# An adaLN transformer block on one core: W_o products of the first last tokens ahead of output sums, VectorE passes over two neighbouring banks, and the plan's constants set anew

## The chip, the cores and the metric

The kernel runs on one core of a Trainium2 chip. A core has five engines with instruction streams of their own: TensorE (PE, matrix products), VectorE (DVE), ScalarE (ACT, exponentials and GELU), GpSimd (POOL) and SyncE (SP, which here only issues DMA transfers). They wait for each other through semaphores; each works its own stream off in order. TensorE writes its results into PSUM, eight banks of 128 partitions x 512 fp32 columns. The metric is the device time of one execution in microseconds, lower is better. Of several executions the median is given.

## The reference, cut to what matters

One sequence of 2048 tokens, width 512, 32 heads of 16, a feed-forward width of 1376:

```python
mod = (silu(c) @ w_mod).reshape(...)                  # sa, ca, ga, sb, cb, gb
h = layernorm(x) * (1 + ca) + sa
q, k, v = split(h @ wqkv)                             # 32 heads of 16
p = softmax(q @ k.T * 16 ** -0.5)
x = x + ga * ((p @ v) @ wo)
h = layernorm(x) * (1 + cb) + sb
x = x + gb * (gelu(h @ w1 + b1) @ w2 + b2)
```

The bulk is attention: for each head 2048 x 2048 scores, their exponentials, and the sums of these with v.

## The kernel before, in words

**Tiling.** A unit of attention `qi` (32 of them) is one block of 512 query tokens, one chunk of eight heads, and one half of these heads, four at a time; the last four units (`halved`) take two halves of 256 tokens instead. A unit has 16 key tiles of 128 keys, and a key tile has four rows (heads): one row is a score product of 32 x 128 by 32 x 512 (`qk`, L922) into one bank. `order` lists all (unit, key tile) pairs, 512 in number.

**Two ways to an exponential.** ScalarE takes two rows at once from banks 0 and 1 (tile `pA`) or 3 and 4 (`pB`), L1291. Some of the key tiles (those listed in `DKT`) go to VectorE and GpSimd instead: VectorE adds a constant to the score and writes int16 (`p_pass`, L1362), a number whose bits read as fp16 are already close to 2**score; three more copies of the tile (`emit_shift`), shifted by constants, are made on VectorE (L1333) or GpSimd (L1339), and products with scaled copies of v (`VV`) sum the four into a better exponential. These rows use the four banks 2, 5, 6 and 7 (`flex`), which they share with output sums and with all other products (`jobs`). A tile of this kind costs four passes, three shifts and 16 products of output sums where ScalarE's way costs two exponentials and four.

**Output sums.** `pv_issue` (L1086) issues a group of four products, one for each row and 32 columns of TensorE; in the halved units the group is eight products of 256 columns. When a unit's sums are complete, VectorE copies them out (L1398), a chain of small DMAs brings the denominators to where they are needed (SP queue: L1419, L1427, L1455, L1465), and GpSimd multiplies (L1477) into `OT`.

**The plan.** The order of all engines' instructions is written out by a planner inside the kernel, when it is built: it keeps a clock for each engine with a price for each kind of work, takes the engine whose clock is lowest, and asks `pe`, `act`, `dve` or `pool` what to issue. Its choices hang on constants. `jobs` (products into a free bank, then an evacuation) and `tasks` (work of another engine) become due when the position in `order` reaches their gate: projections of k and q (`K_GATE`, `Q_GATE`), W_o products (`X1_GATE`), the first and second feed-forward product of a block (`U_GATE`, `OUT_GATE`; `U2_GATE`, `OUT2_GATE` for the third block). `D_AHEAD` and `D_WAIT` say how early and with how much room before the next score group TensorE may issue rows for VectorE alone, `OPEN_N` how many finished exponentials a unit's sums need before they get a bank, `POOL_MIN` how much other work VectorE must have before GpSimd takes a shift, `D_STOP` how many key tiles of a unit must be left. `X_LEAD` moves the position that gates see. `TURNS` sets such constants for one of 64 turns, a turn being half a unit. Time does not enter when the kernel runs: only the order and the semaphores do.

`pe` asks in turn: scores for ScalarE, a bank for a unit's sums, rows for VectorE, then either a step of an open job (`px`) or a group of sums (`pf`) if it ends before the next scores are due. L1191 decides between the last two.

**The end.** For the last block of 512 tokens the first 256 are handled early: the jobs `xA` (eight W_o products for each of the two token tiles) make the residual, then statistics on VectorE (L281, L286), a root on GpSimd (L291, L292), the norm (L782), and two transposing DMAs (L509) into `ha`. For the other 256 tokens the jobs `z` issue the W_o products of three of the four head chunks (`Z_GATE` says when); the fourth follows when the last unit is done. After the last exponential `last_tail` writes a fixed order: VectorE's chain for the last unit (from L1634), with the feed-forward products of the first 256 tokens (L668) as fillers between its steps. `GAPS` says how many fillers go into each gap.

Of the kernel before, what the change touches and what calls it, by code (L numbers as in the profile page):

```python
# [34 lines left out]
VOFF = 16  # L35
VEW = VOFF + H * HS + 16

TURNS = {29: {'D_AHEAD': 0.3}, 30: {'D_AHEAD': 0.3}, 31: {'D_AHEAD': 0.3}, 32: {'D_AHEAD': 0.3}, 47: {'OPEN_N': 10}, 48: {'OPEN_N': 10}, 60: {'D_STOP': 5}, 61: {'D_STOP': 5}, 62: {'D_STOP': 5}, 63: {'D_STOP': 5}}
TURN = 2
DKT = (3, 7, 11, 13, 14, 15)  # L40
NV = 4
# [3 lines left out]
T_BUFS = 5  # L45
P_BUFS = 5
D_FROM = 0
D_AHEAD = 0.1
D_STOP = 4

INF = 1e18
# [30 lines left out]
START = 11.4  # L82
WARM = (16, 0, 0)
Q_POOL = False
PAIR = False
K_GATE = (-1.7, 0.25)
Q_GATE = -1.1
X1_GATE = (0.3, 1.3)
U_GATE = (1.7, 5.0)
OUT_GATE = (5.0, 7.9)  # L90
OPEN_N = 14
LN1_DMA = (2, 3)
LN2_DMA = True
# [1 line left out]
POOL_MIN = 1.0  # L95
D_WAIT = 0.5
# [1 line left out]
TIE = True  # L98
SEARCH = None
NARROW = False  # L100
GAPS = (10, 4, 0, 12, 2, 3, 8, 4)
NHQ = 4
N2_ENG = DV
NHC = NC - NHQ // 2
MMH = 0.25
SP_DH = (0.5, 1.75)
XA_AT = 30.5
U2_GATE = (1.7, 5.0)
OUT2_GATE = (4.6, 7.2)
LOAD_AT = (2, 3)  # L110
D_END = 6
BULK_LEFT = 8
Z_GATE = 0.2


def bf16_round(v):
# [47 lines left out]
def adaln_block(ctx: ExitStack, tc: tile.TileContext, A_x, A_wqkv, A_wo, B_x, B_w1, B_b1, B_w2, B_b2,  # L164
# [386 lines left out]
    for ch in range(1, NC):  # L551
        for b in range(NQB):
            add_k(ch, b, 2 * ch + K_GATE[0] + K_GATE[1] * b)
        add_q(ch, 0, 2 * ch + Q_GATE)
    for b in range(1, NQB):
        for ch in range(NC):
            add_q(ch, b, 8 * b + 2 * ch + Q_GATE)

# [126 lines left out]
    def add_tail(b):  # L685
# [35 lines left out]

        u_gate, out_gate = (U2_GATE, OUT2_GATE) if b == NQB - 2 else (U_GATE, OUT_GATE)
        for fc in range(NFC):
# [97 lines left out]
    st = {"ap": 0, "cur": None, "mode": None, "unit": 0, "lastpe": 0.0, "expd": 0, "extra": 0.0}  # L821

    V = dict(D_AHEAD=D_AHEAD, D_STOP=D_STOP, OPEN_N=OPEN_N, D_WAIT=D_WAIT, POOL_MIN=POOL_MIN, X_LEAD=0.0)
    base = dict(V)
    turn = [-1]

    def next_turn():

        n = st["ap"] * TURN // 16
        if n > turn[0]:  # L830
            turn[0] = n
            V.update(base)
            if SEARCH is not None:
                SEARCH(n, V)
            V.update(TURNS.get(n, {}))

# [33 lines left out]
    xopen = []  # L870
# [266 lines left out]
    def x_mode():  # L1137
        return xopen[0].mode
# [14 lines left out]
    def pe(now):  # L1153
        if issue_unit(now):
            return True
        if open_o(now):
            return True
        x_open(now)
        dl = INF
        if more_units():  # L1160
            u = st["unit"]
            tf = unit_free[u] if unit_free[u] < INF else max(T[AC], now) + EXP_BUSY[unit_cap[u]] + 0.16
            if tf > now:
                dl = max(tf, act_dry() - 0.56)

        def fits(dur, mode):
            return now + (SWITCH if mode != st["mode"] else 0.0) + dur <= dl + 0.03

        sel = pv_pick(now)
        full = len(sel) == 4  # L1170
        dve_idle = T[DV] + 0.6 * (len(dbanks) + sum(1 for x in evacs if x.ready < now + 0.3)) <= now + V["D_AHEAD"]
        if dve_idle and fits(MM, "row") and (dl - now > V["D_WAIT"] or T[DV] <= now and not dbanks):
            banks = bank_for_d(now)
            n = 0
            avoid = []
            while banks and n < 2 and want_d(now, len(banks)):
                r = d_next(now, avoid)
                if r is None:
                    break
                s = now + (SWITCH if st["mode"] != "row" else 0.0)  # L1180
                d_issue(r, s, banks.pop(0))
                avoid.append(r)
                n += 1
            if n:
                pe_start(now, "row", MM, "drow")
                return True
        px = bool(xopen) and fits(xopen[0].cost, x_mode())
        pf = full and fits(MM, "col")
        if not more_units():
            px = px and not pf  # L1190
        if px and not (pf and (pv_pressure() or (x_mode() == "full" and st["mode"] == "col" and not xopen[0].k))):  # L1191
            x_step(now)
            return True
        if pf:
            pv_issue(now, sel)
            return True
        if px:
            x_step(now)
            return True
        idle = now - st["lastpe"]  # L1200
        if sel and fits(MM, "col") and idle > 0.12:
            pressure = pv_pressure() or any(claimed[e[1]] == NKT for _, e in sel)
            if pressure:
                pv_issue(now, sel)
                return True
        if idle > 0.15 and fits(MM, "col") and fill(now):
            return True
        if idle > 0.3 and now > st["extra"] + 0.3:
            extra_fill(now)
        return False  # L1210
# [12 lines left out]
    def pv_pressure():  # L1223
        return any(sl.slots[sl.i][0] for sl in rings) or bool(ring_t.slots[ring_t.i][0]) \
            or bool(ring_u.slots[ring_u.i][0])
# [124 lines left out]
    def p_pass(now):  # L1350
# [3 lines left out]
        n = 1  # L1354
        if PAIR and dbanks and dbanks[0][0] <= now and dbanks[0][1] == i + 1 and dbanks[0][2] is d \
                and dbanks[0][3] == r + 1:
# [236 lines left out]
    def last_tail():  # L1593
# [46 lines left out]
        nc.vector.reciprocal(out=rt, in_=den)  # L1640
        gap(GAPS[0])
        for t in range(2):
# [12 lines left out]
        rs = ln_root(mv, 2)  # L1655
        gap(GAPS[3])
        hns = [otp.tile([P, 512], BF16, name="OT") for _ in range(2)]
# [195 lines left out]
```

## Time and profile before

| | |
|---|---|
| median of 3 runs | 746.65 us (746.38 to 748.83) |
| profiled execution | 745.1 us, span 743.1 us |
| busy: ScalarE, TensorE, VectorE, GpSimd | 717.6, 726.9, 681.9, 422.7 us |
| granted TensorE clock | 1.00 |
| first and last exponential's start | 13.04 and 716.17 us |
| exponentials / int16 passes / shifts on VectorE and GpSimd | 736 / 576 / 240 and 192 |

The span is the time from the first to the last instruction; the execution holds some microseconds around it. A group of instructions in the profile is given with its line, engine, operation, output and inputs, its count, its busy time and the mean of one in ns, and the idle time of its engine in front of it with what ended it. Busy times of matmuls and of ScalarE overlap with those of their neighbours. In the timeline the columns are start, length, and the instruction with its count; a bracket at the end tells the idle time before it.

### The profile page before, as it was taken

What the parts mean: (1) busy time and instruction counts of PE and PEld (TensorE: products, weight loads), DVE (VectorE), ACT (ScalarE), POOL (GpSimd) and SP (SyncE); (2) the same over time, 40 slices, a digit from 0 to 9 for tenths busy, and PEclk for the clock granted to TensorE, in tenths of its full rate; (3) what the DMA queues carried; (4) which work ended last, traced back from release to release, by engine and by line L of the source; (5) the groups of instructions that cost most, each with busy time, mean ns of one, the idle gap of its engine ahead of it and who ended that gap; (6) DMA issues with size and microseconds to landing.
All of it is one profiled execution on the core that took longest, in us unless ns stands there. A gap on an engine that the chain in (4) does not pass through costs nothing.

```text
span 743.1 us, 22093 instructions
## 1 busy us (share of the span) xinstructions
PE 726.9 (98%) x9043; PEld 237.0 (32%) x9046; DVE 681.9 (92%) x1188; ACT 717.6 (97%) x775; POOL 422.7 (57%) x263
## 2 busy tenths in 40 slices
PE   8999999999999999999999999999999999999998
PEld 3323323232333222222222222322232222434455
DVE  8958899999999999999999999999999999989973
ACT  4999999999999999999999999999999999999993
POOL 3102756766565566676777465765667668653610
PEclk9999999999999999999999999999999999999999
DMA  8600101021120100000100200000010200010110
GB/s 275 169 13 2 25 4 24 22 56 48 45 65 11 38 10 23 7 16 24 53 17 8 45 5 15 11 18 24 18 50 5 46 10 9 19 33 15 43 26 31
DMA packets 42859, 25.57 MB, mean 34 GB/s; under 512 B 27609, under 2 KB 37906, under 8 KB 42754
## 3 DMA queue, kind: packets, MB, share of 16 engines
q1 hardware_dynamic: 41938, 23.01, 11.9%
q8 instruction: 72, 1.18, 0.7%
q10 hardware_dynamic: 816, 1.12, 0.4%
q14 instruction: 33, 0.27, 0.1%
HBM read 16.58 MB, written 2.61 MB: 26 GB/s over the span
## 4 chain that ended last, share of the span: by engine, by line
ACT 49%; PE 37%; issue 9%; DVE 4%; POOL 1%; DMA 0%; SPq 0%; DVEq 0%; ACTq 0%; POOLq 0%
ACT pA L1291 24%; ACT pB L1291 24%; PE PS L1086 12%; PE PS L922 12%; PE PS L254 8%; PE PS L668 3%; DVE t L1333 1%; POOL t L1339 1%; DVE t L1362 1%; PE PS L259 1%; ACT uG L728 1%; DVE qm L341 1%; ACT L1291 0%; DMA hT<-OT 0%; PE PS L1103 0%
## 5 line engine op out<-in xcount | busy, mean ns | idle before, releaser
L1339 POOL TENSOR_SCALAR t<-t 128x2048 int16<-128x2048 int16 x192 | 363.7, 1901 | 242.9 <-DVE t L1333 108.9
L1291 ACT ACTIVATE pA<-PS 128x1024 bf16<-128x1024 f32 x368 | 396.0, 1076 | 2.5 <-PE PS L922 2.1
L1291 ACT ACTIVATE pB<-PS 128x1024 bf16<-128x1024 f32 x368 | 396.6, 1078 | 0.1
L1362 DVE TENSOR_SCALAR t<-PS 128x512 int16<-128x512 f32 x576 | 370.5, 680 | 26.1 <-PE PS L922 23.2
L922 PE MATMUL PS<-qm,kT 32*128 32x512 bf16 x2048 | 304.6, 383 | 6.9 <-ACT pA L1291 3.2
L1086 PE MATMUL PS<-t,VV 128*32 128x512 f16 (+1 forms) x1956 | 225.1, 359 | 2.4 <-POOL t L1339 2.1
L922 PEld LDWEIGHTS <-kT 32*128 32x128 bf16 x2048 | 86.4, 91 | 285.0 <-issue 281.0
L1333 DVE TENSOR_SCALAR t<-t 128x2048 int16<-128x2048 int16 x240 | 175.5, 757 | 0.5 <-PE PS L1086 0.2
L1086 PE MATMUL PS<-pA,VE 128*32 128x512 bf16 (+1 forms) x826 | 168.4, 361 | 0.0
L1086 PE MATMUL PS<-pB,VE 128*32 128x512 bf16 (+1 forms) x826 | 164.3, 361 | 0.0
L1086 PE MATMUL PS<-t,VE 128*32 128x512 f16 (+1 forms) x652 | 133.6, 359 | 1.0 <-DVE o_sb L1398 1.0
L1086 PEld LDWEIGHTS <-VE 128*32 128x32 bf16 x2304 | 70.1, 94 | 76.9 <-issue 71.7
L1086 PEld LDWEIGHTS <-VV 128*32 128x32 bf16 x1956 | 65.0, 95 | 59.5 <-issue 53.0
L254 PE MATMUL PS<-h2T,W 128*32 128x512 bf16 x528 | 42.8, 383 | 0.0
L254 PE MATMUL PS<-W,uG 128*32 128x512 bf16 x528 | 40.3, 383 | 0.0
L1103 PE MATMUL PS<-kT,zeros 128*32 128x512 bf16 x296 | 28.3, 383 | 0.0
L1477 POOL TENSOR_TENSOR OT<-o_sb,rb 128x512 bf16<-128x512 f32 (+1 forms) x17 | 20.0, 1177 | 13.3 <-DVE t L1333 11.6
L719 DVE TENSOR_SCALAR uG<-PS,b1c 128x512 bf16<-128x512 f32 x33 | 24.5, 741 | 1.6 <-PE PS L254 1.2
L291 POOL TENSOR_SCALAR rs<-mv 128x4 f32<-128x4 f32 (+1 forms) x10 | 4.3, 427 | 36.5 <-DVE mv L286 36.0
L341 DVE TENSOR_SCALAR qm<-PS,qmask 128x512 bf16<-128x512 f32 x32 | 22.6, 741 | 2.2 <-PE PS L254 2.2
L254 PE MATMUL PS<-hT,W_k 128*32 128x512 bf16 x256 | 21.2, 383 | 0.5 <-DVE hT L324 0.5
L254 PE MATMUL PS<-hT,W_q 128*32 128x512 bf16 x256 | 20.9, 383 | 0.0
(129 smaller groups left out, 365.1 us busy)
## 6 DMA issues: line engine op xcount, KB each, us to landing
rb<-d SPq DMA_DIRECT2D x112, 32.0 KB
W_m<-in_w_mod_dram SPq DMA_DIRECT2D x2, 1024.0 KB
out_dram<-ob SPq DMA_DIRECT2D x15, 128.0 KB
o_sb<-o SPq DMA_DIRECT2D x56, 32.0 KB
xb<-in_A_x_dram SPq DMA_DIRECT2D x3, 512.0 KB
xr<-in_A_x_dram SPq DMA_DIRECT2D x3, 512.0 KB
W<-in_B_w_dram SPq DMA_DIRECT2D x4, 344.0 KB
W<-in_B_w_dram SPq DMA_DIRECT2D x5, 256.0 KB
```

The costliest lines, as they stand in the source:

```text
L254: nc.tensor.matmul(out=ps[32 * g:32 * g + 32, :], lhsT=lhsT[:, 32 * g:32 * g + 32], rhs=rhs, start=start, stop=stop)
L341: nc.vector.tensor_scalar(out=qm[(b, ch)][:, par, :], in0=ps, scalar1=qmask[:, par:par + 1], scalar2=None, op0=ALU.mult)
L668: nc.tensor.matmul(out=ps, lhsT=lhsT, rhs=rhs, start=start, stop=stop)
L719: nc.vector.tensor_scalar(out=X["u"][:, fc, :], in0=bank(ps), scalar1=late["b1c"][:, fc:fc + 1], scalar2=None, op0=ALU.add)
L922: nc.tensor.matmul(out=dst, lhsT=kT[rows, ch, kt * P:(kt + 1) * P], rhs=rhs, start=True, stop=True)
L1086: nc.tensor.matmul(out=bank(O[qi])[32 * r:32 * r + 32, cs], lhsT=w, rhs=rhs[:, cs], start=(n == 1 and not halved(qi)), stop=last and (pr = ...
L1103: nc.tensor.matmul(out=bank(O[qi])[32 * r:32 * r + 32, :], lhsT=zeros[:, 0:32], rhs=kT[:, 0, 0:512], start=False, stop=False)
L1291: nc.scalar.activation(out=t[:, 0:n, :], in_=PS[:, b0:b0 + n, :], func=ACT.Exp, scale=math.log(2.0) / STEP)
L1333: nc.vector.tensor_scalar(out=t16[:, rs, :], in0=d["tile"][:, rs, :], scalar1=float(MJ[j]), scalar2=None, op0=ALU.add)
L1339: nc.gpsimd.tensor_scalar(out=t16[:, rs, :], in0=d["tile"][:, rs, :], scalar1=1.0, scalar2=float(MJ[j]), op0=ALU.mult, op1=ALU.add)
L1362: nc.vector.tensor_scalar(out=d["tile"][:, r:r + n, :], in0=PS[:, i:i + n, :], scalar1=T_BIAS, scalar2=0.0, op0=ALU.add, op1=ALU.max)
L1477: nc.gpsimd.tensor_tensor(out=ot[:, 0:w], in0=o[:, 0:w], in1=rb[:, 0:w], op=ALU.mult)
```

## The change

Three parts. L1191: a job `xA` that is open is no longer held back by a group of sums that is ready. `PAIR`: where two neighbouring rows of one tile lie ready in two neighbouring banks, `p_pass` takes both in one instruction of 1024 columns. And constants: gates, `D_AHEAD`, `GAPS`, `Z_GATE`, and another `TURNS` table.

```diff
-TURNS = {29: {'D_AHEAD': 0.3}, 30: {'D_AHEAD': 0.3}, 31: {'D_AHEAD': 0.3}, 32: {'D_AHEAD': 0.3}, 47: {'OPEN_N': 10}, 48: {'OPEN_N': 10}, 60: {'D_STOP': 5}, 61: {'D_STOP': 5}, 62: {'D_STOP': 5}, 63: {'D_STOP': 5}}
+TURNS = {17: {'D_WAIT': 0.8}, 18: {'D_WAIT': 0.8}, 19: {'D_WAIT': 0.8}, 20: {'D_WAIT': 0.8}, 45: {'D_AHEAD': 0.4}, 46: {'D_AHEAD': 0.4}, 37: {'X_LEAD': -0.1}, 38: {'X_LEAD': -0.1}, 39: {'X_LEAD': -0.1}, 40: {'X_LEAD': -0.1}, 55: {'D_WAIT': 0.7, 'OPEN_N': 16}, 56: {'D_WAIT': 0.7, 'POOL_MIN': 0.8, 'OPEN_N': 16}, 57: {'D_WAIT': 0.7}, 58: {'D_WAIT': 0.7, 'X_LEAD': 0.1}, 59: {'X_LEAD': 0.0}, 60: {'D_WAIT': 0.7, 'X_LEAD': 0.0}, 61: {'D_WAIT': 0.7, 'X_LEAD': 0.0}, 62: {'D_WAIT': 0.7, 'X_LEAD': 0.0}, 63: {'D_WAIT': 0.7}, 51: {'D_WAIT': 0.7}, 52: {'D_WAIT': 0.7}, 53: {'D_WAIT': 0.7}, 54: {'D_WAIT': 0.7}}
...
-D_AHEAD = 0.1
+D_AHEAD = 0.2
...
-PAIR = False
-K_GATE = (-1.7, 0.25)
-Q_GATE = -1.1
+PAIR = True
+K_GATE = (-1.7, 0.22)
+Q_GATE = -1.2
 X1_GATE = (0.3, 1.3)
-U_GATE = (1.7, 5.0)
-OUT_GATE = (5.0, 7.9)
+U_GATE = (1.7,4.8)
+OUT_GATE = (4.6, 7.8)
...
-GAPS = (10, 4, 0, 12, 2, 3, 8, 4)
+GAPS = (10, 4, 0, 12, 3, 3, 7, 4)
...
-U2_GATE = (1.7, 5.0)
-OUT2_GATE = (4.6, 7.2)
+U2_GATE = (1.7,4.6)
+OUT2_GATE = (4.6,7.4)
...
-Z_GATE = 0.2
+Z_GATE = 0.6
...
-        if px and not (pf and (pv_pressure() or (x_mode() == "full" and st["mode"] == "col" and not xopen[0].k))):
+        if px and (xopen[0].name[0] == "xA" or not (pf and (pv_pressure() or (x_mode() == "full" and st["mode"] == "col" and not xopen[0].k)))):
             x_step(now)
             return True
```

The line of `p_pass` that `PAIR` switches on stood in the kernel before:

```python
        if PAIR and dbanks and dbanks[0][0] <= now and dbanks[0][1] == i + 1 and dbanks[0][2] is d \
                and dbanks[0][3] == r + 1:
```

## The prediction

> **What bounds the kernel now.** I read the page's totals first, then the waits by engine, then busy time by stage, and last the timeline of ScalarE and TensorE. Page and waits (waited for: us in total, times, longest):
>
> ```profile
> span 743.1 us, 22093 instructions
> PE 726.9 (98%) x9043; PEld 237.0 (32%) x9046; DVE 681.9 (92%) x1188; ACT 717.6 (97%) x775; POOL 422.7 (57%) x263
> ...
> L1339 POOL TENSOR_SCALAR t<-t 128x2048 int16<-128x2048 int16 x192 | 363.7, 1901 | 242.9 <-DVE t L1333 108.9
> L1291 ACT ACTIVATE pA<-PS 128x1024 bf16<-128x1024 f32 x368 | 396.0, 1076 | 2.5 <-PE PS L922 2.1
> L1291 ACT ACTIVATE pB<-PS 128x1024 bf16<-128x1024 f32 x368 | 396.6, 1078 | 0.1
> ...
> L1362 DVE TENSOR_SCALAR t<-PS 128x512 int16<-128x512 f32 x576 | 370.5, 680 | 26.1 <-PE PS L922 23.2
> ```
> ```profile
> PE PS L922 <- ACT pA L1291: 3.2, 13, 0.6
> PE PS L1086 <- POOL t L1339: 2.1, 6, 0.5
> DVE t L1362 <- PE PS L922: 23.2, 63, 1.1
> ```
>
> ScalarE runs 736 exponentials of two 512-column tiles and hardly idles. The exponentials overlap, so the distance between their starts counts, not their 1.08 us. Stages: before the pause of the first GELU, the first and the last of three such pauses, and what follows the last exponential's start.
>
> ```profile
> 13.04:304.77 291.73, 288.16 (x3379) 87.10 (x3379) 267.28 (x479) 290.51 (x315) 156.02 (x98) 1.00 0.16 42
> 304.77:313.39 8.62, 7.51 (x100) 2.54 (x92) 8.37 (x14) 8.56 (x6) 5.89 (x4) 1.00 0.02 4
> ...
> 646.13:654.75 8.62, 8.22 (x167) 4.25 (x159) 8.40 (x13) 8.56 (x5) 4.27 (x3) 1.00 0.02 5
> ...
> 716.17:743.10 26.93, 23.11 (x171) 15.29 (x170) 12.26 (x30) 12.90 (x27) 0.94 (x2) 1.00 0.10 29
> ```
>
> The columns are length, then busy time of TensorE, its weight loads, VectorE, ScalarE and GpSimd. From the first exponential's start to the last one's are 716.17 - 13.04 = 703.13 us: 735 distances, three of them pauses of 8.62. What sets an ordinary distance stands in TensorE's timeline, here around one long one:
>
> ```profile
> 366.46 0.39 PE L922 MATMUL PS<-qm,kT 32*128 32x512 bf16 x3
> 366.79 0.39 PE L1086 MATMUL PS<-pA,VE 128*32 128x512 bf16 x2
> ...
> 367.01 0.38 PE L1086 MATMUL PS<-t,VE 128*32 128x512 f16 x1
> ...
> 367.23 0.38 PE L1086 MATMUL PS<-t,VE 128*32 128x512 f16 x1
> ...
> 367.55 0.39 PE L922 MATMUL PS<-qm,kT 32*128 32x512 bf16 x4
> ```
> ```profile
> 367.07 1.03 ACT L1291 ACTIVATE pA<-PS 128x1024 bf16<-128x1024 f32 x1
> 368.11 1.02 ACT L1291 ACTIVATE pB<-PS 128x1024 bf16<-128x1024 f32 x1
> 369.03 1.02 ACT L1291 ACTIVATE pA<-PS 128x1024 bf16<-128x1024 f32 x1
> ```
>
> Between two score groups (366.46, 367.55) lie three groups of output products 0.22 apart. The next exponential starts 0.56 after its scores, and the distance is 1.04; the following one is 0.92. I counted the groups between neighbouring score groups in the program's order and held them against all distances. The first and last with three groups, of 148 outside the pauses:
>
> ```profile
> 16.67 1.05 ACT L1291 ACTIVATE pA<-PS 128x1024 bf16<-128x1024 f32 x1
> 17.58 1.07 ACT L1291 ACTIVATE pB<-PS 128x1024 bf16<-128x1024 f32 x1
> ...
> 709.79 1.15 ACT L1291 ACTIVATE pA<-PS 128x1024 bf16<-128x1024 f32 x1
> 710.73 1.12 ACT L1291 ACTIVATE pB<-PS 128x1024 bf16<-128x1024 f32 x1
> ```
>
> These 148 average 0.971 (143.7 in all); the other 584 (a lone 2.06 near the start among them) average (703.13 - 25.86 - 143.7) / 584 = 0.914. So ScalarE bounds most of the span, and TensorE stretches it where three groups lie in one interval.
>
> **The change, part by part.** The retuned constants reorder the whole plan, so I price what its order contains, counted in the built program.
>
> *Exponentials.* 734 instead of 736: one more score tile goes the integer way (145 instead of 144; 580 rows instead of 576). Three-group intervals: 146 instead of 149 (one of the 149 lay in a pause). With the prices above: 25.86 + 146 x 0.971 + 584 x 0.914 = 701.4, against 703.1 from the same rounded prices: two ordinary-to-long distances less, -1.9. Against it, the three-group intervals hold more changes between TensorE's tile shapes: those with one, two, three changes number 15, 82, 49, where they were 36, 83, 30 and averaged 0.953, 0.971, 0.992. That mix costs +0.8 in full. Ends -1.9 and -1.1; I take -1.5, the middle, since the shape changes may only mark a crowded stretch.
>
> *The extra tile on the others.* Three more GpSimd tables (195 instead of 192) and three more half-width product groups, 0.23 each; GpSimd is 57% busy, and the groups are in the interval count. The zero products put into idle TensorE slots make 80 groups instead of 81. Nothing more is added to the sum; if the tables had no cover, they would cost GpSimd 3 x 1.9 us.
>
> *GpSimd's tables.* A late table delays products, then scores, then the exponential:
>
> ```profile
> 144.36 1.03 ACT L1291 ACTIVATE pB<-PS 128x1024 bf16<-128x1024 f32 x1
> 145.53 1.02 ACT L1291 ACTIVATE pA<-PS 128x1024 bf16<-128x1024 f32 x1
> ```
> ```profile
> 144.64 0.40 PE L1086 MATMUL PS<-t,VV 128*32 128x512 f16 x4 [0.20 <-POOL t L1339]
> ```
>
> That distance is 1.17, 0.26 above 0.91, and there are 6 such waits. In the new order 4 tables are first read within two exponentials of their issue, where 10 were. Ends 0 and -1.6 (all six gone); I take half, -0.8.
>
> *Passes over two banks.* 42 pairs replace 84 of the passes; 496 single ones stay. No pair is in this trace. Widths of VectorE reading scores' banks, and two passes back to back:
>
> ```profile
> 705.53 1.27 DVE L1362 TENSOR_SCALAR t<-PS 128x512 int16<-128x512 f32 x2
> ...
> 737.52 0.69 DVE L1691 TENSOR_TENSOR ob<-PS,xr 128x512 bf16<-128x512 f32 x1 [1.76 <-PE PS L668]
> 738.72 0.42 DVE L1691 TENSOR_TENSOR ob<-PS,xr 128x256 bf16<-128x256 f32 x1 [0.51 <-PE PS L668]
> ```
>
> 256 more elements cost 0.27, so a pair takes about 0.69 + 0.54 = 1.23 where two take 1.27: 42 x 0.04 = 1.7 us of VectorE at best, and 42 x 0.09 = 3.8 us more of it if a pair cost twice the mean single pass (1.36). I take 1.23, the row of one instruction. VectorE waits 23.2 us for scores already, so either is covered: 0 in the sum; without that cover it would be a gain of 1.7 or a loss of 3.8. What it can cost: the first row of a pair is handed over 0.54 later than by a single pass, and so is its bank, for which TensorE's next scores wait. By the row, the second bank comes at 1.23 instead of 1.27 and a tile's tables need all four rows anyway: 0.
>
> The Trainium skill, "PSUM — Partial Sum Buffer", section "PSUM bank collisions raise a hardware error", says to guard PSUM by bank and quadrant with semaphores: TensorE may not refill a bank while VectorE still reads the pair. No run here shows it for pairs; by the row the sum stays, by that rule it is that of the third rival below.
>
> *W_o products first.* The condition on L1191 puts the eight products of each of the two jobs ahead of output sums. By the order, the second result's add comes 9 exponentials before the last instead of 7; but four shift passes of about 0.6 now stand before the two normalisations, which come 4 and 3 before the last (5 and 4 before), and the two transposing DMAs 4 and 2 (both 4). On SP the x load of the last half moves from 20 to 9 exponentials before the last, ahead of the transposes; its issue takes 0.40 and the transposes come five exponentials later, so it holds nothing up; its data are needed only by the adds after the last exponential.
>
> ```profile
> 696.62 0.40 SPq L804 DMA_DIRECT2D xr<-in_A_x_dram  x1
> ```
>
> *Tail.* Rows of the end:
>
> ```profile
> 710.56 0.41 PE L1086 MATMUL PS<-t,VV 128*32 128x256 f16 x8
> 710.79 0.28 PE L1086 MATMUL PS<-pA,VE 128*32 128x256 bf16 x2
> ...
> 716.45 1.03 PE L668 MATMUL PS<-W_o,OT 128*128 128x512 bf16 x4 [0.16 <-issue]
> 717.40 0.29 PE L1086 MATMUL PS<-pA,VE 128*32 128x256 bf16 x2
> ...
> 718.31 2.54 PE L668 MATMUL PS<-hT,W 128*128 128x256 bf16 x20 [0.17 <-DMA hT<-OT]
> ...
> 726.63 0.59 PE L668 MATMUL PS<-W,hT 128*128 128x512 bf16 x2
> 727.36 1.91 PE L668 MATMUL PS<-h2T,W 128*128 128x256 bf16 x16
> ```
> ```profile
> 714.07 0.73 DVE L782 TENSOR_SCALAR OT<-hT,mv,rs 128x512 bf16<-128x512 bf16 x2 [0.92 <-POOL rs L292]
> ```
>
> From the last exponential's start TensorE is busy 23.11 of 26.93 us, so the end follows from when the feed-forward products start (718.31, after a wait of 0.17 for the transposes). The new order leaves 33 half-width output products behind the last scores instead of 13: 20 / 8 x 0.23 = +0.58; six W_o products stand there in both. Of that, 0.16 idle before 716.45 and the 0.17 wait absorb 0.33. The transposes: the statistics come two exponentials earlier, so the 0.92 wait for GpSimd goes, and three shift passes of 0.6 take its place; the second transpose lands at about the same time after the last exponential and is hidden under the later TensorE. The gaps' new filler (three products instead of two behind the transposes) goes into the 0.14 between 727.22 and 727.36. Ends 0 and +0.75; I take +0.3.
>
> *Sum.* -1.5 - 0.8 + 0.3 = -2.0: span 741.1, profiled execution 743.1 (its 745.1 holds 2.0 around the span). The median of the three runs is 1.55 above that execution; the prediction carries this over: 746.65 - 2.0 = 744.7. Its own range goes from -1.9 - 1.6 + 0 to -1.1 + 0 + 0.75: 743.1 to 746.3.
>
> **Rivals.** *The tail eats the gain.* Nothing of +0.58 is absorbed, three W_o products of 0.22 that used to run while TensorE waited for the last exponential now follow the sums (+0.66), the mix costs its full +0.8, and the tables' waits stay: -1.9 + 0.8 + 1.2 = +0.1, 746.8. For it: the order shows all of these. Against: the 0.33 of idle time is there.
>
> *Long intervals get cheaper.* 23 three-group intervals that follow one with a single group average 0.930. If half of the 146 go that way because TensorE is less late before them, 73 x 0.04 = 2.9 more: 741.8. Against: such pairs number 22 in the new order.
>
> *Pairs hand over late: slower.* TensorE works in order, so each wait for a pair's bank or first row costs ScalarE up to the 0.26 of a late table. The gain is gone at 8 of 42 pairs, no-change is left behind at 17 ((2.0 + 2.24) / 0.26); half of them give -2.0 + 21 x 0.26 = +3.5, 750.1. For it: VectorE's 63 waits for scores say banks are tight, and TensorE has little slack in long intervals. Against: passes first read within one exponential number 6, where 14 did.
>
> **How the numbers follow.** A measurement can tell about 0.3%, 2.24 us: faster is below 744.4, slower above 748.9. Forecast 0.40 (its range lies across 744.4: 0.18 faster, 0.22 same), tail 0.20 (same), cheaper intervals 0.17 (faster), late pairs 0.23 (slower). Faster 0.35, same 0.42, slower 0.23. The range 741.6 to 749.6 leaves out some 0.06 of the fast side and half of the late pairs.
>
> **What would show it.** Right: 734 exponentials, the last one starting near 714.2 to 714.7; pauses still 8.62; TensorE's waits for GpSimd at 3 or so; pairs near 1.2 us; feed-forward products starting about 2.4 us after the last exponential's start, with no wait for the transposes. Wrong: waits of TensorE's scores for VectorE's passes, distances above 1.1 after pairs, pairs well over 1.3 us, or pauses longer than 8.62 because the first sums' results come late.

## The result and the profile after

The changed kernel takes 744.5 us, median of 12 runs (743.42 to 746.97); the kernel before took 746.62 beside it (745.38 to 748.83, 12 runs). The ratio is 0.9971, 95% interval 0.9957 to 0.9985: 1.1 to 3.2 us less, about 2.2. The prediction had said 744.7. A second measurement of the same kernel gave 743.96 and 0.9976 [0.9964, 0.9987]. The profiled execution took 744.46, span 742.6.

The page of the kernel after: span, then two rows of engines' busy times, then groups of instructions.

```profile
span 742.6 us, 22110 instructions
PE 724.4 (98%) x9066; PEld 235.7 (32%) x9066; DVE 680.9 (92%) x1150; ACT 716.8 (97%) x773; POOL 429.4 (58%) x266
...
L1339 POOL TENSOR_SCALAR t<-t 128x2048 int16<-128x2048 int16 x195 | 369.1, 1901 | 238.7 <-DVE t L1333 124.0
L1291 ACT ACTIVATE pA<-PS 128x1024 bf16<-128x1024 f32 x367 | 393.6, 1073 | 2.2 <-PE PS L922 2.0
L1291 ACT ACTIVATE pB<-PS 128x1024 bf16<-128x1024 f32 x367 | 393.9, 1073 | 0.0
```

Its groups with the shapes apart, VectorE's passes:

```profile
L1362 DVE TENSOR_SCALAR t<-PS 128x512 int16<-128x512 f32 x496 | 321.5, 679 | 22.9 <-PE PS L922 20.0 <-issue 0.3
...
L1362 DVE TENSOR_SCALAR t<-PS 128x1024 int16<-128x1024 f32 x42 | 51.0, 1213 | 2.7 <-PE PS L922 2.2 <-issue 0.2
```

Its waits (in total, times, longest):

```profile
DVE t L1362 <- PE PS L922: 22.2, 52, 1.4
...
PE PS L922 <- ACT pB L1291: 3.9, 15, 1.0
...
PE PS L922 <- ACT pA L1291: 2.7, 10, 0.9
...
PE PS L1086 <- POOL t L1339: 1.5, 4, 0.8
...
PE PS L306 <- DMA W_m<-in_w_mod_dram: 0.8, 1, 0.8
```

Busy time by stage: up to the first pause, the first and last pause, and from the last exponential's start (columns as before).

```profile
13.94:303.23 289.29, 285.25 (x3355) 86.64 (x3355) 263.89 (x460) 288.04 (x312) 159.21 (x99) 1.00 0.16 41
303.23:311.78 8.55, 7.14 (x101) 2.64 (x97) 7.95 (x12) 8.49 (x6) 6.57 (x5) 1.00 0.01 3
644.17:652.77 8.60, 8.18 (x147) 3.85 (x138) 8.26 (x13) 8.55 (x5) 3.52 (x3) 1.00 0.03 8
715.89:742.60 26.71, 23.39 (x192) 15.53 (x182) 12.17 (x30) 12.97 (x27) 0.94 (x2) 0.99 0.10 28
```

The stages show what the ends of the execution hide. From the first exponential's start to the last one's are 715.89 - 13.94 = 701.95 us, 1.18 less than before; from there to the end 26.71 instead of 26.93, 0.2 less (the span is printed to 0.1 us, so the end is good to 0.05). Together that is 1.4. The 0.90 by which the first exponential comes later (13.94 against 13.04) is not the change's: it goes with the last wait above, for the load of `W_m` ahead of everything that was changed; two kernels below that differ from this one only later, after_split and after_oldgaps, begin at 13.04 and 13.12.

All distances between neighbouring exponentials' starts, in the classes of the prediction (three-group intervals; ordinary ones under 1.1; strays of 1.1 or more, without the 2.06 near the start, which stayed at 2.07), each as count, mean and sum:

| | before | after |
|---|---|---|
| three groups | 148, 0.971, 143.7 | 146, 0.976, 142.5 |
| ordinary | 577, 0.909, 524.5 | 581, 0.911, 529.3 |
| strays | 6, 1.171, 7.0 | 2, 1.167, 2.3 |
| three pauses | 25.84 | 25.70 |

Two distances fewer at the ordinary 0.909 are -1.82; what the three-group intervals take beyond 0.909 rose from 9.2 to 9.8, +0.63; the strays' excess fell by 1.05; and the ordinary distances, longer by 0.002 each, gave 1.19 back. With -0.14 from the pauses that is -1.18.

Do the strays that went away come from late tables of GpSimd? The kernel before has six waits of TensorE for such a table: the one at 144.64 that the prediction shows, and these.

```profile
480.11 0.40 PE L1086 MATMUL PS<-t,VV 128*32 128x512 f16 x4 [0.49 <-POOL t L1339]
482.88 0.40 PE L1086 MATMUL PS<-t,VV 128*32 128x512 f16 x4 [0.48 <-POOL t L1339]
495.75 0.40 PE L1086 MATMUL PS<-t,VV 128*32 128x512 f16 x4 [0.22 <-POOL t L1339]
585.15 0.40 PE L1086 MATMUL PS<-t,VV 128*32 128x512 f16 x4 [0.51 <-POOL t L1339]
649.51 0.30 PE L1086 MATMUL PS<-t,VV 128*32 128x256 f16 x4 [0.16 <-POOL t L1339]
```

Three of them lie in pauses (475.36 to 483.98 and 646.13 to 654.75), where ScalarE runs no exponentials, and the one at 495.75 has distances of 0.90 and 0.94 around it. Only two lie at a stray: 144.64 at 1.17 and 585.15 at 1.28. Together these two exceed 0.909 by 0.63. The other four strays hold no wait for a table. Of the four waits of the kernel after, two lie in pauses (310.06 and 476.81), and none lies at a stray.

The start of the end, from the last scores for ScalarE to the first feed-forward product, before and then after:

```profile
715.57:718.31 2.74, 2.41 (x19) 0.84 (x20) 0.40 (x1) 2.72 (x3) 0.10 (x1) 1.00 0.48 96
715.27:718.13 2.86, 2.86 (x44) 1.32 (x41) 0.50 (x1) 2.84 (x3) 0.00 (x0) 1.00 0.29 56
```

TensorE was idle for 0.33 of the 2.74 us, and for none of the 2.86. It is busy 0.45 us longer there, and the products start 0.1 later after the last exponential's start.

### The profile page after: what moved, and what is told of

It reads as the page before. It is cut to its first block, busy times and chain, and to the rows that moved or that the text cites. A ratio compares the mean times of both kernels' runs of the same rounds, so it can differ in the third digit from the quotient of the medians.

```text
span 742.6 us, 22110 instructions
## 1 busy us (share of the span) xinstructions
PE 724.4 (98%) x9066; PEld 235.7 (32%) x9066; DVE 680.9 (92%) x1150; ACT 716.8 (97%) x773; POOL 429.4 (58%) x266
## 3 DMA queue, kind: packets, MB, share of 16 engines
q10 hardware_dynamic: 816, 1.12, 0.4%
## 4 chain that ended last, share of the span: by engine, by line
ACT 48%; PE 39%; issue 8%; DVE 3%; DMA 1%; POOL 0%; ACTq 0%; POOLq 0%; DVEq 0%
ACT pB L1291 23%; ACT pA L1291 23%; PE PS L1086 14%; PE PS L922 13%; PE PS L254 9%; PE PS L668 2%; ACT uG L728 1%; DMA W_m<-in_w_mod_dram 1%; DVE t L1362 1%; DVE qm L341 0%; PE PS L1103 0%; ACT L1291 0%; DVE t L1333 0%; POOL t L1339 0%; DVE st L281 0%
## 5 line engine op out<-in xcount | busy, mean ns | idle before, releaser
L1339 POOL TENSOR_SCALAR t<-t 128x2048 int16<-128x2048 int16 x195 | 369.1, 1901 | 238.7 <-DVE t L1333 124.0
L1362 DVE TENSOR_SCALAR t<-PS 128x512 int16<-128x512 f32 (+1 forms) x538 | 369.9, 721 | 25.6 <-PE PS L922 22.2
L1086 PE MATMUL PS<-pA,VE 128*32 128x512 bf16 (+1 forms) x822 | 163.3, 362 | 0.0
L1086 PE MATMUL PS<-t,VE 128*32 128x512 f16 (+1 forms) x660 | 130.9, 357 | 0.0
L254 PE MATMUL PS<-W,uG 128*32 128x512 bf16 x528 | 42.5, 383 | 0.0
L1103 PE MATMUL PS<-kT,zeros 128*32 128x512 bf16 x320 | 30.5, 382 | 0.0
```

Source lines behind the costliest of these rows:

```text
L254: nc.tensor.matmul(out=ps[32 * g:32 * g + 32, :], lhsT=lhsT[:, 32 * g:32 * g + 32], rhs=rhs, start=start, stop=stop)
L1086: nc.tensor.matmul(out=bank(O[qi])[32 * r:32 * r + 32, cs], lhsT=w, rhs=rhs[:, cs], start=(n == 1 and not halved(qi)), stop=last and (pr = ...
L1103: nc.tensor.matmul(out=bank(O[qi])[32 * r:32 * r + 32, :], lhsT=zeros[:, 0:32], rhs=kT[:, 0, 0:512], start=False, stop=False)
L1339: nc.gpsimd.tensor_scalar(out=t16[:, rs, :], in0=d["tile"][:, rs, :], scalar1=1.0, scalar2=float(MJ[j]), op0=ALU.mult, op1=ALU.add)
L1362: nc.vector.tensor_scalar(out=d["tile"][:, r:r + n, :], in0=PS[:, i:i + n, :], scalar1=T_BIAS, scalar2=0.0, op0=ALU.add, op1=ALU.max)
```

## The experiments

The table holds what the profiles of all kernels show, in the terms that the experiments turn on: exponentials; from the first one's start to the last one's ("region"); and, after the last one's start, when the feed-forward products begin, when VectorE's last chain (L1634) begins, when TensorE's last products (`W,uG`) begin, and the end of the span (good to 0.05). Ratios are to the kernel before, measured beside each. The gates, `D_AHEAD` and `Z_GATE` were not set back by themselves, so what each of them is worth is not known.

| kernel | exponentials | region | products | L1634 | `W,uG` | end | median, ratio [95%] |
|---|---|---|---|---|---|---|---|
| before | 736 | 703.13 | 2.14 | 1.74 | 18.77 | 26.93 | 746.62 |
| after | 734 | 701.95 | 2.24 | 1.74 | 18.56 | 26.71 | 744.50, 0.9971 [0.9957, 0.9985] |
| after_again | 734 | 701.97 | 2.24 | 1.74 | 18.55 | 26.70 | 743.96, 0.9976 [0.9964, 0.9987] |
| after_split | 734 | 702.32 | 2.24 | 1.74 | 18.56 | 26.94 | 744.42, 0.9996 [0.9982, 1.0010] |
| after_oldcond | 734 | 701.96 | 3.31 | 1.73 | 19.35 | 27.53 | 745.17, 0.9995 [0.9982, 1.0007] |
| after_oldgaps | 734 | 701.98 | 2.24 | 1.74 | 18.77 | 27.00 | 744.19, 0.9982 [0.9967, 0.9996] |
| after_nopair | 740 | 707.90 | 2.72 | 1.52 | 18.74 | 27.19 | 749.95, 1.0054 [1.0040, 1.0068] |
| after_oldturns | 738 | 706.31 | 2.53 | 2.34 | 19.15 | 27.68 | 748.94, 1.0039 [1.0025, 1.0054] |
| after_noturns | 736 | 704.32 | 3.54 | 1.70 | 19.76 | 27.98 | 748.30, 1.0037 [1.0023, 1.0051] |
| after_dup12 | 746 | 715.38 | 2.25 | 1.76 | 18.57 | 27.01 | 756.20, 1.0133 [1.0110, 1.0155] |
| after_fill2 | 734 | 705.27 | 3.07 | 1.74 | 19.11 | 27.27 | 748.01, 1.0023 [1.0008, 1.0039] |
| before_xa | 736 | 703.13 | 2.39 | 2.51 | 19.54 | 27.74 | 746.44, 1.0008 [0.9991, 1.0025] |
| before_pair | 738 | 705.03 | 2.58 | 2.33 | 19.36 | 30.48 | 751.13, 1.0064 [1.0042, 1.0086] |
| before_pair_again | 738 | 704.73 | 2.69 | 2.33 | 19.36 | 30.76 | 752.10, 1.0091 [1.0075, 1.0108] |

### The same kernel again

No edit.

> The changed kernel once more, unchanged, beside the kernel before on one chip. The traces so far say that two executions differ in when the first load of w_mod lands (first exponential at 12.9 to 15.5 us), and that what follows repeats to about 0.1 us. My theory: first exponential's start to last one's 701.95 +- 0.1, tail 26.7 +- 0.1, whatever the first start; ratio to the kernel before 0.998 (1.4 us less from the first exponential on), within 0.9971 to 0.999. Rival (the gain of 2.1 us is all in what follows the first exponential): a ratio of 0.997 and a length below 701.5.

Region and end came out within 0.02 of the first execution. What differed is the start: the first exponential began at 16.43 instead of 13.94, and the waits of this execution name the load.

```profile
PE PS L306 <- DMA W_m<-in_w_mod_dram: 1.8, 1, 1.8
```

Over all kernels the first exponential began between 12.91 and 16.43. The region repeats within 0.02 us here and within 0.30 in the two executions of before_pair, so differences of the region above some 0.3 can be read; differences between the times of single executions cannot.

### The pairs, issued as singles in the same order

```diff
-        nc.vector.tensor_scalar(out=d["tile"][:, r:r + n, :], in0=PS[:, i:i + n, :], ...)
+        for x in range(n):
+            nc.vector.tensor_scalar(out=d["tile"][:, r + x, :], in0=PS[:, i + x, :], ...)
```

> The changed kernel with its whole order kept, but each of the 42 passes over two banks issued as two passes over one bank, back to back. My theory (VectorE is covered, ScalarE's exponentials and TensorE's long intervals set the time): the same time as the changed kernel, 744.5 +- 0.7; VectorE's busy time about 2 us longer (42 x (1.27 - 1.21)), TensorE's waits for VectorE's passes unchanged. Rival 1 (a pair hands its first row and bank over late): faster by up to 42 x 0.26 = 11 us, visibly at least 2 us, with fewer waits of scores for VectorE. Rival 2 (the pairs themselves bring the gain): slower by about 2 us, 746.6.

The region grew by 0.37 us, hardly more than two executions of one kernel can differ. The median, 744.42, is that of after (744.50, 743.96); the kernel before was at 745.23 beside it, so the ratio is 0.9996 where after's are 0.9971 and 0.9976, and the intervals just overlap. By the profile the pairs themselves bring 0.4 at most; the times leave room for more. The profile's groups after the edit:

```profile
L1363 DVE TENSOR_SCALAR t<-PS 128x512 int16<-128x512 f32 x580 | 372.2, 679 | 24.2 <-PE PS L922 21.5
```

VectorE is not relieved by them: 496 singles and 42 pairs take 321.5 + 51.0 = 372.5 us, 580 singles 372.2 (busy times overlap), not the 2 us more that was expected. The pairs do not hand over late by any amount that shows: without them the region is no shorter.

### The plan without pairs

```diff
-PAIR = True
+PAIR = False
```

> The changed kernel with PAIR off, so that the plan is made anew without two-bank passes: 740 exponentials instead of 734 and 137 three-group intervals instead of 146. My theory prices the order: (740 - 4 - 137) x 0.914 + 137 x 0.971 = 680.3, against 675.3 for the changed kernel by the same prices: +5.0, 749.5 +- 1. It says that pairs pay through the plan: VectorE's time that they free lets the planner give VectorE three more key tiles. Rival (pairs cost TensorE waits, so the plan without them runs closer to its order): 745 to 747. Rival (TensorE's total work bounds, fewer integer tiles mean fewer products): 742 or less.

+5.95 us in the region, 1.0054 in time. The planner prices a pair at 1.135 us and two singles at 2 x 0.602, and the order that it makes with pairs sends three more key tiles to VectorE, each of which otherwise costs ScalarE two exponentials: 740 exponentials without pairs, 734 with them. So nearly all that the pairs bring in this plan comes through the order, although VectorE itself is not relieved by them. The region grew by 0.95 more than the count of exponentials and three-group intervals gives (+5.0).

### The former `TURNS`, and none

```diff
-TURNS = {17: {'D_WAIT': 0.8}, ... 54: {'D_WAIT': 0.7}}
+TURNS = {29: {'D_AHEAD': 0.3}, ... 63: {'D_STOP': 5}}
```

> The changed kernel with the old TURNS table: 738 exponentials, 141 three-group intervals. My theory by the prices: (738 - 4 - 141) x 0.914 + 141 x 0.971 = 678.9, 3.4 above the changed kernel: 747.9 +- 1. Rival (the table works by taking away waits for GpSimd's tables, not by the number of exponentials): the distances above 1.1 us rise from 3 to 8 or more and explain the difference. Rival (the table does nothing): 744.5.

```diff
-TURNS = {17: {'D_WAIT': 0.8}, ... 54: {'D_WAIT': 0.7}}
+TURNS = {}
```

> The changed kernel with an empty TURNS table: 736 exponentials instead of 734, 138 three-group intervals instead of 146 (with one, two, three shape changes 21, 73, 44), 57 half-width groups of sums behind the last scores instead of 33. My theory (count of exponentials and of three-group intervals at after's own prices, 0.912 and 0.976): region +2 x 0.912 - 8 x 0.064 = +1.3, that is 703.3; tail +24 / 8 x 0.23 = +0.7 at most if TensorE's idle time there is used up: 27.0 to 27.4; time about 746.2. Rival A (the former tables lose in addition through late tables or passes, as with the old TURNS, where the region came out 0.8 to 1.0 above the count): 704.2 or more. Rival B (the turns do nothing that the count does not show, and the tail hides the sums): 745.8.

The regions grew by 4.36 and 2.37, where the counts gave 3.4 and 1.3, so both times Rival A of the second run fits. With the old table seven distances are 1.1 or more and with none six, where after has three (the pauses and the one near the start left out); the three-group intervals average 0.983 and 0.982 instead of 0.976. The end without a table is 27.98, later than the 27.0 to 27.4 that was expected. So the new table is worth two exponentials against none, four against the old one, and about 1 us each time that the count does not show.

### What an exponential and a third group cost

Every 60th exponential issued twice, with the same output:

```diff
+                ndup[0] += 1
+                if ndup[0] % 60 == 30:
+                    nc.scalar.activation(out=t[:, 0:n, :], in_=PS[:, b0:b0 + n, :], func=ACT.Exp, ...)
```

> The changed kernel with every 60th exponential issued twice, the same instruction on the same data: 12 more on ScalarE, nothing else moved. My theory (ScalarE bounds nearly everywhere): 12 x 0.91 = +10.9, first to last exponential 712.9 +- 0.7. Rival (TensorE's work bounds and ScalarE has slack to give back in the intervals that follow): +6 or less, since TensorE would catch up after each.

12 more exponentials lengthened the region by 13.43, 1.12 each, more than the 10.9 expected. In its waits, TensorE's scores wait for the second copy (L1296), which reads the same banks once more:

```profile
PE PS L923 <- ACT pB L1296: 8.7, 12, 1.2
```

So TensorE does not make up for an added exponential in what follows: the price is a whole one, and 0.2 more. The 0.2 goes with the banks that the copy holds, so it is not shown for an added exponential with scores of its own.

A group of products of zeros, added to sums, in 41 intervals that held two groups; the output is the same:

```diff
+        if nunit[0] - 1 in EXTRA and O:
...
+                for r in range(4):
+                    nc.tensor.matmul(out=bank(O[oq])[32 * r:32 * r + 32, :], lhsT=zeros[:, 0:32],
+                                     rhs=kT[:, 0, 0:512], start=False, stop=False)
```

> The changed kernel with a group of zero products (added to a running sum) put into 41 two-group intervals whose neighbours hold at most two, which makes 187 three-group intervals of 146. My theory (a third group costs only what does not fit under the exponential): 41 x (0.971 - 0.912) = +2.4, first to last exponential 704.4 +- 0.8. Rival (TensorE bounds): each costs its whole 0.22, +9.1. Rival (a third group costs nothing by itself, long intervals are long for other reasons): 702.0.

+3.32 in the region. Those 41 distances went from 0.911 to 0.980, and the ones behind them grew by 0.021: 0.09 for each added group by the distances, 0.08 by the region. It confirms what the prediction read off the timeline: a third group takes 0.22 of TensorE, lengthens its own distance by 0.07 and the next one by 0.02.

### W_o products first, undone in the new plan and done alone in the old one

```diff
-        if px and (xopen[0].name[0] == "xA" or not (pf and (...))):
+        if px and not (pf and (...)):
```

> The changed kernel with only the old condition on L1191: W_o products of xA wait again for output sums. The order differs from the 721st of 734 exponentials on; the statistics come 5 instead of 7 exponentials before the last, both norms 3 before it. My theory: the tail is set by TensorE's work behind the last scores, the transposes are hidden; 744.5 +- 0.5, the feed-forward products start 2.2 to 2.4 us after the last exponential's start, as in the changed kernel (2.24). Rival (the earlier W_o products bring the tail's gain): the feed-forward products wait for the transposes again, start 0.3 to 1 us later, and the time is 745 to 745.5.

The region stayed (701.96), the end came some 0.8 later. The timelines of TensorE and VectorE in this kernel, whose last exponential starts at 717.47:

```profile
720.78 1.48 PE L668 MATMUL PS<-hT,W 128*128 128x256 bf16 x12 [0.91 <-DMA hT<-OT]
```
```profile
716.45 0.73 DVE L782 TENSOR_SCALAR OT<-hT,mv,rs 128x512 bf16<-128x512 bf16 x2 [0.61 <-POOL rs L292]
```

and of the kernel after, whose last exponential starts at 715.89:

```profile
716.38 0.82 PE L668 MATMUL PS<-W_o,OT 128*128 128x512 bf16 x3
717.47 0.82 PE L668 MATMUL PS<-W_o,OT 128*128 128x512 bf16 x3
718.13 2.35 PE L668 MATMUL PS<-hT,W 128*128 128x256 bf16 x20
```
```profile
713.05 0.40 DVE L782 TENSOR_SCALAR OT<-hT,mv,rs 128x512 bf16<-128x512 bf16 x1
713.37 0.68 DVE L1333 TENSOR_SCALAR t<-t 128x2048 int16<-128x2048 int16 x1
713.98 0.40 DVE L782 TENSOR_SCALAR OT<-hT,mv,rs 128x512 bf16<-128x512 bf16 x1
```

Without the edit the norms start 1.02 before the last exponential, with it 2.84 and 1.91 before. The two transposes (SP, L509) are issued 1.8 us earlier, and the 0.91 of waiting goes. The theory that the edit brings nothing fell, and the rival held.

The same edit in the kernel before:

> The kernel before with the condition of L1191 alone. 736 exponentials and 149 three-group intervals with the same shape changes as before. My prediction credited this edit with 0; the run of after without it showed the tail 0.8 longer, with TensorE 0.91 late on the transposes. In the kernel before that wait is 0.17. My theory now: what the edit is worth is that wait and no more, so here region 703.1 (within 0.4), the wait for the transposes gone, the tail 26.8 (-0.17), time -0.2, not to be told from no change. Rival A: it is worth 0.8 in this plan too, tail 26.1. Rival B: three shift passes of VectorE now stand before the normalisation and make it late, so the transposes land later: wait 0.3 or more, tail 27.2 or more.

The region is 703.13 as before, TensorE's products do not wait for the transposes, and still the end came some 0.8 later. TensorE and VectorE of this kernel, last exponential at 717.46:

```profile
718.12 1.47 PE L668 MATMUL PS<-W_o,OT 128*128 128x512 bf16 x6
719.52 0.40 PE L1086 MATMUL PS<-pB,VE 128*32 128x256 bf16 x4
719.85 1.37 PE L668 MATMUL PS<-hT,W 128*128 128x256 bf16 x11
```
```profile
713.07 0.41 DVE L782 TENSOR_SCALAR OT<-hT,mv,rs 128x512 bf16<-128x512 bf16 x1
713.39 1.89 DVE L1333 TENSOR_SCALAR t<-t 128x2048 int16<-128x2048 int16 x3
719.97 0.72 DVE L1634 STREAM_TRANSPOSE rb<-PS 128x512 f32<-128x512 f32 x1 [4.69 <-PE PS L1086]
```

And VectorE of the kernel before, last exponential at 716.17:

```profile
717.91 0.72 DVE L1634 STREAM_TRANSPOSE rb<-PS 128x512 f32<-128x512 f32 x1 [3.10 <-PE PS L1086]
```

In this order all six W_o products stand ahead of the last sums, and run from 718.12 to 719.52, past the end of the last exponential. The last sums come 2.06 after its start (1.23 before), and VectorE's last chain 2.51 instead of 1.74: +0.77, which is what the last products lose (19.54 against 18.77). Rival B's size came, by another way than it said. So by the profiles the edit makes the one plan 0.8 us faster and the other 0.8 slower; the times of before_xa (1.0008) cannot tell that from nothing.

A rule for this tail can be fitted to the rows of the table. With the old `GAPS` the last products start 18.77 after the last exponential, with the new 18.56, plus whatever L1634 is later than 1.74: +0.77 (before_xa), +0.59 (before_pair), +0.59 for +0.60 (after_oldturns). When the first products are late instead, part of the delay is absorbed: 0.28 of it, if that is taken from after_oldcond (3.31 - 2.24 - 0.28 = 0.79). With this 0.28 the rule gives after_fill2's 0.55 to the hundredth, and it misses after_noturns by 0.18.

### The former `GAPS`

```diff
-GAPS = (10, 4, 0, 12, 3, 3, 7, 4)
+GAPS = (10, 4, 0, 12, 2, 3, 8, 4)
```

> The changed kernel with only GAPS as before: (10, 4, 0, 12, 2, 3, 8, 4), that is, two instead of three feed-forward products in the gap behind the transposes and eight instead of seven in the last one. The plan up to the last exponential is the same. My theory after the profiles: the third filler takes the idle slot between the transposes and the following products, so that the last second-layer products start 0.21 sooner after the last exponential (18.56 in after, 18.77 in before). Expected here: region from first to last exponential 702.0 as in after (within 0.3), the last feed-forward products starting 18.77 after the last exponential, tail 26.9, time about 0.2 above after's (744.7). Rival A, the prediction's step: the filler takes 0.14 of idle time at most and the rest lies elsewhere: 18.65 or less. Rival B: the 0.21 comes from the order of the products before it and not from GAPS: 18.56.

The last products start at 18.77, as the theory said. TensorE of this kernel (last exponential at 715.10) and of after (715.89):

```profile
725.56 0.59 PE L668 MATMUL PS<-W,hT 128*128 128x512 bf16 x2
726.28 1.91 PE L668 MATMUL PS<-h2T,W 128*128 128x256 bf16 x16
728.03 1.89 PE L668 MATMUL PS<-W,hT 128*128 128x512 bf16 x8
```
```profile
726.36 0.81 PE L668 MATMUL PS<-W,hT 128*128 128x512 bf16 x3
727.08 1.91 PE L668 MATMUL PS<-h2T,W 128*128 128x256 bf16 x16
728.82 1.67 PE L668 MATMUL PS<-W,hT 128*128 128x512 bf16 x7
```

The products on `h2T` start 0.72 after the fillers in both, whether these are two or three: the third was free, and the seven that follow are one fewer. In time 0.2 cannot be told from nothing (0.9982 against 0.9971 and 0.9976).

### The pairs alone

```diff
-PAIR = False
+PAIR = True
```

in the kernel before, twice.

> The kernel before with only PAIR on: the plan is made anew and has 738 exponentials (736) and 126 three-group intervals (149). My theory by the prices: (738 - 4 - 126) x 0.914 + 126 x 0.971 = 678.0 against 677.4 for the kernel before: +0.6, same within 0.3%; pairs alone bring nothing, they pay only with the constants set for them. Rival (pairs by themselves make the kernel faster): 2 us less than before. Rival (pairs make TensorE wait for banks): 2 us more, with TensorE's waits for VectorE's passes above 2 us in total.

> The kernel before with the pairs alone, a second time, since the parts of its first execution add up to less than its times: from first to last exponential +1.9, the chain after the last exponential +0.59 (VectorE's L1634 starts 2.33 after the last exponential's start instead of 1.74), but 2.96 more lay between the start of the last products and the end (11.12, where the other kernels take 8.15 to 8.23). Theory: those 2.96 are a late landing of the last output transfer in that one execution; the order gives 705.0 and 19.36 to the last products' start again, then 8.2, tail 27.5, and a median about 2.5 above before's. Rival: the end is longer in this order each time: 11 again, tail 30.5, median about 5 above.

Pairs without the new constants make the kernel slower: 738 exponentials where 736 were, the region +1.9 and +1.6, L1634 0.59 later; and 3 us more between the last products' start and the end (11.12 and 11.40; 8.15 to 8.53 in all other kernels). The theory that this was a late transfer in one execution fell. The DMA queues of the second execution from 744.5 to its end, 40 slices of 0.1 us:

```profile
DMA  0200900000000000000000000000000000000000
GB/s 0 82 0 0 164 0 0 0 0 0 0 0 0 0 0 0 0 0 0 0 0 0 0 0 0 0 0 0 0 0 0 0 0 0 0 0 0 0 0 0
...
q8 instruction: 1, 0.02, 2.3%
q14 instruction: 1, 0.01, 0.6%
```

and of the kernel before from 739.1 to its end:

```profile
DMA  7996700005950000000001882020000003009000
GB/s 276 369 358 205 205 0 0 0 0 174 292 139 10 0 10 10 5 5 10 0 0 61 261 261 72 0 82 0 0 0 0 0 0 82 0 0 164 0 0 0
```

The last two packets that start are of the instruction queues in both. In the kernel before the span ends 0.3 behind their starts; here it goes on for some 3.5 us, after the output was written. The closing instructions of the streams (L1848) show which engine is late: count, durations in ns, first and last start, for TensorE (PEldq) and then SyncE (SPq), in this execution and then in the kernel before.

```profile
L1848 PEldq DRAIN  x2: 8/8/8, 747.7 to 748.1; - x2
L1848 SPq DRAIN  x3: 7/7/13, 744.5 to 748.0; - x3
```
```profile
L1848 PEldq DRAIN  x2: 8/8/8, 742.2 to 742.7; - x2
L1848 SPq DRAIN  x3: 7/7/13, 742.3 to 742.6; - x3
```

TensorE's stream has passed its last instruction of L1712 at 744.2 and comes to the first closing one 3.5 us later, where the kernel before needs 0.2; in the first execution of before_pair it goes from 746.4 to 749.6. The other engines are there by 744.5 and wait. What TensorE's stream waits for is not named. The last packet above, of the instruction queue q8 from 744.9 on, would fit a late load of its instructions, but no run shows that. The two executions show that the delay comes with this program.

## Why the prediction was right, and where it was not

The time was right (744.7 for 744.5), and its own steps gave -2.0, where first exponential to end shows -1.4. The measured 2.2, with its interval of 1.1 to 3.2, holds both. That the forecast came within 0.2 us is partly luck: none of the three terms of the sum was right by itself, and their misses are made up for by something that the profiles do not show in these stages. The starts may do it: the wait for `W_m` moved single executions by more than the whole change, but only profiled executions show their starts.

- **Exponentials and three-group intervals, -1.5 said, -1.2 came.** 734 exponentials, as counted, for -1.82. The step that failed is the choice of the middle: the mix of intervals cost nearly its full price. With before's means per class (0.953, 0.971, 0.992) the new mix of 15, 82, 49 gives 142.5, and 142.5 were measured. Whether the shape changes themselves cost this or mark crowded stretches is not shown. Another cut of the same intervals carries over as well: by whether TensorE issues score rows for VectorE ahead of the next scores, before's means are 0.948 without (67 intervals) and 0.990 with (81), and the new 46 and 100 at these means give 142.6. (The comparison figure of the prediction, 703.1 "from the same rounded prices", should read 703.3; its -1.9 is right.)
- **GpSimd's tables, -0.8 said, none came in sum.** The step that failed is the price of 0.26 for each of six waits: it was read from one wait, and three of the six lay in pauses and a fourth at ordinary distances. Only two lay at a long distance, and their 0.63 did go. The waits went from 6 to 4 (2.1 to 1.5 us), the strays' excess in all fell by 1.05, and what the others of them came from is open. Against it, the ordinary distances grew by 0.002, +1.19 over 581 of them. That one caused the other is not shown, and what lengthened the ordinary distances is open: issuing the pairs as singles made the ordinary and stray distances no shorter either (0.9128 on average, against 0.9119).
- **Passes over two banks, 0 said.** Right as instructions: 1.213 us for the predicted 1.23, and 0.4 in the region at most. No wait of TensorE's scores names a pass of VectorE. The 0 for work that is covered left out, though, what the pairs do through the plan: without them it has six exponentials more and is 5.95 us longer in the region. The counts of the built order held that worth already, so the sum didn't miss it; an account by parts would have.
- **W_o products first, nothing credited.** Wrong as a price for the edit: by the profile it is worth 0.8 us in the new plan. The prediction compared the norms' places in the two orders, and between these nothing was to be had but the wait of 0.17; in the new plan without the edit the norms come later, and TensorE waits 0.91 for the transposes.
- **Tail, +0.3 said, -0.2 came.** The feed-forward products start 2.24 after the last exponential's start (2.4 said; 2.14 before): the idle 0.33 was taken up whole, as counted, but TensorE's work there grew by 0.45 and not by 0.58. And "the end follows from when the feed-forward products start" failed: by the rule fitted above 0.28 of a delay there is absorbed, VectorE's chain from L1634 counts as well, and it did not move (1.74). The filler in the 0.14 wait, credited 0, was worth 0.21.
- **What would show it.** The last exponential started at 715.89, not at 714.2 to 714.7: 0.90 of that is the later start, the rest the first two steps above. Pauses 8.55 to 8.60 (8.62 said), table waits 4 (3 or so said), no wait for the transposes (right).
- **Rivals.** *The tail eats the gain*: it had the mix at full cost and the tables without gain, both right, but its 1.2 of tail didn't come: the idle time took most of the added sums, and the filler brought 0.21. *Cheaper long intervals*: no, 0.976 against 0.971. *Late pairs*: no; distances of 1.1 or more (the pauses and the one near the start left out) fell from 8 to 3, and the same order with singles was no faster. The rule cited there from the Trainium skill ("PSUM — Partial Sum Buffer", "PSUM bank collisions raise a hardware error"), that a bank is guarded until its reader is done, is not contradicted: in this trace no wait of the scores for a pass shows, so the banks of the pairs were free in time.

## What to carry to other kernels

When constants of a planner change, count the built order (instructions of the bounding engine, intervals by what they hold) with prices from the trace of before: here the counts gave the differences of the region to within 1.3 us, always too low for the slower orders (3.4 for 4.36, 5.0 for 5.95, 1.3 for 2.37, 0.6 for 1.9). Before you credit a stall that goes away, look up where each of its waits lies: here three of six lay in pauses and cost nothing. And don't price an edit of an order by itself: the same condition changed the end by -0.8 us in one plan and +0.8 in the other, and the pairs the region by -6 in one and +2 in the other. For differences of 1 to 2 us in 745, compare stages from the first to the last instruction of the bounding engine, as the start of an execution varies by more.

## What the runs showed of the hardware that was not expected

- The first exponential's start varied from 12.91 to 16.43 us between executions, 13.94 and 16.43 for one and the same kernel, with the wait for one weight load; from there on that kernel repeated within 0.02 us in 702.
- An exponential that reads the same two banks a second time cost 1.12 us, not the 0.91 of the distances; the next scores waited for it, 8.7 us in 12 waits.
- A pass of 1024 columns takes 1.213 us; two of 512 behind each other cover 1.27 in the timeline, and 580 singles keep VectorE busy no longer in sum than 496 and 42 pairs.
- In one order TensorE's stream came to its closing instructions 3.2 and 3.5 us after its last other instruction, in both executions; in the kernel before it took 0.2. The cause is open.
